# A Nyström attention and two MLP layers: the first batch's loads and the order of its scores, Newton's iteration and weight conversion

## The chip, the cores and the metric

The kernel runs on one core of a Trainium2 chip. The metric is the device time of one execution in microseconds (us). Each core has TensorE (PE in the profile, its weight loads PEld), VectorE (DVE), ScalarE (ACT), GpSimd (POOL), and SyncE (SP), which here issues all input and weight transfers.

## The reference

```python
# q, k, v: (4, 8, 576, 64) float32; 32 landmarks, each the mean of 18 consecutive tokens
q_lm = q.reshape(B, H, m, S // m, D).mean(axis=3);  k_lm likewise
A  = sm(q, k_lm)        # sm: softmax of the scaled products over the last axis
Bm = sm(q_lm, k_lm)
C  = sm(q_lm, k)
Z  = Bm^T / (norm_1(Bm) * norm_inf(Bm) + 1e-6)
for _ in range(6):
    Z = 2 * Z - Z @ Bm @ Z
x = A @ Z @ C @ v                       # per batch and head; heads side by side: (2304, 512)
g = x @ w_gate; x = (g * sigmoid(g) * (x @ w_val)) @ w_out          # 512 -> 1536 -> 512
x = (sigmoid(x @ w2_gate) * (x @ w2_val)) @ w2_out                  # the same shapes
```

## The kernel before

Four batches of 576 tokens are worked on, each in two halves g of four heads. Matmuls of the MLP run on pairs of numbers (a rounded part and the rest), so the float32 weights are loaded as raw bits (tile `raw`) and taken apart into such forms by `convert`: two passes on ACT (L329, L332) and two on DVE (L334, L338) for each piece of 128x512. The 1536 hidden columns go in six chunks c of 256. A chunk's gate and value weights of the first layer are four raw pieces, each loaded by four transfers of 128 KB; its output weights are two pieces, split by L365 and L366.

The work is written as Python generators, each `yield` a step; a scheduler sets the order of the instructions on each engine from the order in which the steps are written and from its own model of durations.

- `front(b, g)` (word F): sums each landmark's tokens (`lm`, on DVE for the very first half, on POOL in six instructions L127 to L132 for all others), turns the inputs on PE (`lt`, `tp`; copied out by ACT L141, L149), forms the landmark scores (`cs`, maximum L170, exponential `e` L175) and the 32x32 landmark matrix (`bm`, then `bs` L186, exponential L187), turns `e` (`et`, `eT` L199), multiplies with v (`cv`, L206), and last forms the scores of all tokens (`as`, L220, L221, exponential L223 into `sx`).
- `back(b)` (word B): scales `bs` by its row sums (L254), copies it into `bc` (L255), gets the norms (L258 to L273: the factor `rr`), then Newton's iteration, six products `nw` on PE with a combination on DVE between them (`rw`: first L288, then L293, L299), turns the result (`ut`, L303), and has the attention matrices normalised and turned by `a_steps` (L229 to L239, into `AH`). Up to now one step of `a_steps` follows each iteration (`step(ga)`).
- `uw_steps` (U) multiplies the converted weights `w` with `ut` (`pu`, split into `uw` by L365, L366); `gv1_steps` (G) makes the gate and value products from `AH` and `uw` (`pg`, `pv`) and `h`; `o1_steps` (O) the output products `po`.
- `load_attn` issues an input's transfer (576 KB), `load_next` that of a later half, `load_to(n)` the raw pieces up to the n-th. `wfill` is a list of weight conversions from which `emit` takes a step between the steps of other words.

The order of the start is the list of words `first`: "F00 F01 B0 I0 F10 U00 G00 F11 J0 O00 B1 ...", where F10 is `front(1, 0)`. From U00 on chunks of the MLP's first layer for batch 0 run while the other batches' attention is worked into them; the second layer follows.

Of the kernel before, what the change touches and what calls it, by code (L numbers as in the profile page):

```python
# [7 lines left out]
F32 = mybir.dt.float32  # L8
F32R = mybir.dt.float32r
U32 = mybir.dt.uint32  # L10
AF = mybir.ActivationFunctionType
ALU = mybir.AluOpType
# [4 lines left out]
def nystrom_moe_kernel(tc, q, k, v, wg1, wv1, wo1, wg2, wv2, wo2, out):  # L17
# [53 lines left out]
    def load_attn(b, which, g):  # L71
        if which == "v":
            t = att.tile([TP, 4, R, D], F32, tag="vin", name=f"vin{b}_{g}", bufs=1)
            nc.sync.dma_start(t, v[b, 4 * g:4 * g + 4].rearrange("h (p r) d -> p h r d", r=R))
        else:
            t = att.tile([P, L, D], F32, tag="in", name=f"{which}in{b}_{g}", bufs=4)
            src = {"q": q, "k": k}[which]
            nc.sync.dma_start(t, src[b, 4 * g:4 * g + 4].rearrange("h (t u) d -> (h t) u d", u=L))
        inq[which, b, g] = t
# [8 lines left out]
    def load_next(b, g, which):  # L88
        i = AORDER.index((b, g)) + (1 if which == "v" else 2)
        if i < len(AORDER):  # L90
            load_attn(AORDER[i][0], which, AORDER[i][1])
# [22 lines left out]
    def front(b, g):  # L114
# [3 lines left out]
        def sm(tag, shape, bufs=2):  # L118
            return small(tag, shape, nm_, bufs)

        def lm_steps(which):
            src = inq[which, b, g]
            lm = sm("lm", [P, 2, D], 1)
# [15 lines left out]
            bdt = sm("bd" + which, [P, 2, P], 1)  # L139
# [104 lines left out]
    def back(b):  # L244

        def sm(tag, shape, bufs=2):
            return small(tag, shape, b, bufs)
# [6 lines left out]
        nc.vector.tensor_tensor(bs, bs, bsm[:, :, None].to_broadcast([P, 2, M]), op=ALU.mult)  # L254
        nc.scalar.copy(BC[:, :, 0:M], bs)  # L255

        bmt = sm("bmt", [P, 2, M])
# [5 lines left out]
        nb = sm("nb", [P, 4, M], 1)  # L263
# [26 lines left out]
        for it in range(5):  # L290
            ps = prod(RW)
            RW2 = sm("rw", [P, 2, 96], 2)
            nc.vector.scalar_tensor_tensor(RW2, RW, 2.0, ps, op0=ALU.mult, op1=ALU.subtract)  # L293
            RW = RW2
            step(ga)
            yield
# [11 lines left out]

    for g in range(2):
        for x in "kqv" if g == 0 else "kq":  # L310
            load_attn(0, x, g)
# [34 lines left out]
    def load_in(layer, c, kk):  # L346
        t = raw_tile()
# [438 lines left out]

    def emit(word, nw=1):
# [10 lines left out]

    wfill.extend(weights(0, c) for c in range(2))
    first = (  # L800
        "F00 F01 B0 I0 F10 U00 G00 F11 J0 O00 B1 I1 U10 G10 J1 F20 O10 U01 G01 "
        "F21 U11 B2+F30 O01 G11 F31 U02 O11 G02 B3 U12 O02 G12 U03 O12 G03 U13 O03 G13"
    )
    for w in first.split():
        emit(w)
# [121 lines left out]
```

## Time and profile before

| | us |
|---|---|
| median of 3 runs (lowest, highest) | 875.0 (874.72, 875.87) |
| profiled execution, whole time | 877.74 |
| its span, first to last instruction | 876.0 |
| TensorE busy | 845.4 (97%) |
| VectorE busy | 661.2 (75%) |
| ScalarE busy | 475.4 (54%) |
| GpSimd busy | 58.8 (7%) |

The profiled execution took 1.7 us more than its span and 2.7 us more than the median. The page's chain of work that ended last gives 86% of the span to TensorE, 8% to VectorE, 3% to ScalarE and 1% to transfers. Times in a timeline are counted from the span's start.

### The profile page before, as it was taken

The page shows a single profiled execution, that of the slowest core. Times are in us where ns is not written, and L with a number is a line of the kernel's source. Part 1 is how long each engine was busy: PE and PEld are TensorE (multiplying, and loading weights), DVE is VectorE, ACT ScalarE, POOL GpSimd, SP SyncE. Part 2 cuts the span into 40 slices and gives each one's busy share as a digit, 9 for nine tenths or more (in the row PEclk, how much of TensorE's full clock was granted, in tenths as well). Part 3 has the DMA queues.
Part 4 walks back from the last instruction along what each step waited for, and adds up shares of the span by engine and source line. Part 5 has one row for each costly group of instructions (what it writes and reads, how often), then busy time and mean ns, then how long its engine had stood idle before and what let it go on. Part 6 is the DMA issues. An engine that isn't in the chain of part 4 may idle for free.

```text
span 876.0 us, 15884 instructions
## 1 busy us (share of the span) xinstructions
PE 845.4 (97%) x6172; PEld 700.8 (80%) x6172; DVE 661.2 (75%) x1295; ACT 475.4 (54%) x967; POOL 58.8 (7%) x90
## 2 busy tenths in 40 slices
PE   6788999999999999999999999999999899999998
PEld 4476777888788888888878888888888778888886
DVE  3889876866976687579998567979779965687655
ACT  5677565455752454247557655556637466455431
POOL 4635231000000000000000000000000000000000
PEclk9789999999999999999999999999999999999999
DMA  7777421021520131014614315335245433232003
GB/s 248 196 196 212 124 63 30 2 73 43 174 77 22 49 97 50 1 62 156 208 57 145 120 59 183 109 132 175 90 144 187 123 113 134 93 120 72 1 25 96
DMA packets 41484, 93.31 MB, mean 107 GB/s; under 512 B 5825, under 2 KB 8897, under 8 KB 41409
## 3 DMA queue, kind: packets, MB, share of 16 engines
q1 hardware_dynamic: 40640, 91.25, 33.4%
q10 hardware_dynamic: 768, 1.05, 0.5%
q8 instruction: 48, 0.79, 0.4%
q14 instruction: 28, 0.22, 0.1%
HBM read 72.88 MB, written 19.40 MB: 105 GB/s over the span
## 4 chain that ended last, share of the span: by engine, by line
PE 86%; DVE 8%; ACT 3%; issue 2%; DMA 1%; SPq 0%; DVEq 0%; ACTq 0%
PE po L65 31%; PE pg L65 21%; PE pv L65 20%; PE pu L65 2%; PE pgr L65 2%; PE pvr L65 2%; PE tp L148 2%; PE nw L65 1%; PE as L65 1%; PE cs L65 1%; DVE cv L334 1%; DVE acc L583 1%; DMA qin<-in_q_dram 1%; PE cv L65 1%; DVE xl L366 1%
## 5 line engine op out<-in xcount | busy, mean ns | idle before, releaser
L65 PE MATMUL po<-wo,h 128*128 128x512 f32 x432 | 109.8, 391 | 0.0
L65 PEld LDWEIGHTS po<-h,wo 128*128 128x128 f32 x480 | 82.7, 188 | 27.9 <-issue 7.5
L65 PE MATMUL po<-h,wo 128*128 128x512 f32 (+1 forms) x480 | 104.2, 373 | 0.2 <-ACT h L365 0.2
L65 PE MATMUL pg<-AH,uw 128*128 128x288 f32 x552 | 95.3, 299 | 1.3 <-ACT uw L365 1.0
L65 PEld LDWEIGHTS po<-wo,h 128*128 128x128 f32 x432 | 80.6, 188 | 17.7 <-DVE oacc L760 0.2
L65 PE MATMUL pv<-AH,uw 128*128 128x288 f32 x552 | 91.8, 297 | 0.5 <-DVE sg L525 0.5
L760 DVE TENSOR_TENSOR oacc<-po,oacc 128x512 f32<-128x512 f32 x90 | 60.0, 684 | 36.2 <-PE po L65 36.1
L65 PEld LDWEIGHTS pg<-AH,uw 128*128 128x128 f32 x552 | 80.4, 188 | 6.4 <-issue 2.5
L65 PEld LDWEIGHTS pv<-AH,uw 128*128 128x128 f32 x552 | 79.0, 188 | 4.0 <-issue 1.7
L329 ACT ACTIVATE cv<-raw 128x512 f32<-128x512 f32 x84 | 56.7, 676 | 35.2 <-DVE st L338 9.4
L65 PE MATMUL po<-hh,wo 128*128 128x288 f32 x256 | 58.9, 310 | 0.0
L334 DVE SCALAR_TENSOR_TENSOR cv<-cv,cv 128x512 uint32<-128x512 uint32 x84 | 58.0, 693 | 0.8 <-ACT cv L332 0.8
L332 ACT ACTIVATE cv<-raw 128x512 uint32<-128x512 uint32 x84 | 55.8, 669 | 3.4 <-DVE wo L366 3.4
L583 DVE TENSOR_TENSOR acc<-po,acc 128x512 f32<-128x512 f32 x64 | 43.5, 686 | 14.8 <-PE po L65 14.4
L528 ACT ACTIVATE sg<-pg 128x288 f32<-128x288 f32 x64 | 26.2, 409 | 49.5 <-PE pg L65 49.5
L65 PE MATMUL pg<-AH,wk 128*128 128x512 f32 x192 | 50.0, 390 | 0.0
L65 PE MATMUL pv<-AH,wk 128*128 128x512 f32 x192 | 49.5, 389 | 0.0
L65 PEld LDWEIGHTS po<-hh,wo 128*128 128x128 f32 x256 | 41.6, 189 | 4.8 <-issue 2.4
L365 ACT CAST h<-h 128x288 fp32r<-128x288 f32 x64 | 27.6, 433 | 30.7 <-DVE h L529 30.6
L366 DVE TENSOR_TENSOR h<-h,h 128x288 fp32r<-128x288 f32 x64 | 29.1, 456 | 17.5 <-ACT h L365 17.1
L65 PEld LDWEIGHTS pv<-AH,wk 128*128 128x128 f32 x192 | 36.0, 188 | 7.5
L65 PEld LDWEIGHTS pg<-AH,wk 128*128 128x128 f32 x192 | 35.7, 188 | 7.4 <-ACT c5g L682 0.2
(206 smaller groups left out, 1773.5 us busy)
## 6 DMA issues: line engine op xcount, KB each, us to landing
raw<-in_moe_w_out_dram SPq DMA_DIRECT2D x36, 512.0 KB, 4.1
raw<-in_moe_w_gate_dram SPq DMA_DIRECT2D x48, 128.0 KB, 3.2
raw<-in_moe_w_val_dram SPq DMA_DIRECT2D x48, 128.0 KB, 3.0
raw<-in_moe_w_gate_dram SPq DMA_DIRECT2D x24, 256.0 KB, 3.0
raw<-in_moe_w_val_dram SPq DMA_DIRECT2D x24, 256.0 KB, 3.8
wkd<-st SPq DMA_DIRECT2D x24, 256.0 KB, 3.2
wtd<-tf SPq DMA_DIRECT2D x12, 512.0 KB, 3.7
st<-wkd SPq DMA_DIRECT2D x24, 256.0 KB, 3.3
```

What stands on the lines that cost most here:

```text
L65: return nc.tensor.matmul(o, l, r, start=start, stop=stop, skip_group_check=True)
L148: nc.tensor.transpose(ps[:, j], flat(src[:, 2 * u:2 * u + 2]), ident)
L329: nc.scalar.activation(t0, hiw.bitcast(F32), AF.Copy, scale=2.0 ** -112)
L332: nc.scalar.activation(u1, low, AF.Copy, scale=0.875 * 2.0 ** -29, bias=0.49)
L334: nc.vector.scalar_tensor_tensor(u1, u0, 3, u1, op0=ALU.logical_shift_left, op1=ALU.bitwise_or)
L365: nc.scalar.copy(hi, x)
L366: nc.vector.tensor_tensor(lo, x, hi.bitcast(F32), op=ALU.subtract)
L528: nc.scalar.activation(sg, pss[0], AF.Silu)
L583: nc.vector.tensor_tensor(sl, ps, sl, op=ALU.add)
L760: nc.vector.tensor_tensor(acc, ps, acc, op=ALU.add)
```

## The change

Six things change.

1. Batch 0 is loaded in the order k0, q0, k1, raw piece 0, v0, q1, v1, raw pieces 1 to 3; all of it stands ahead of batch 1's first input. So that none of it waits for a buffer, v1 and raw piece 3 get places of the `wo` tiles, and the k side's block matrix of half 1 a place of the `CL` tiles.
2. `lm` gets two buffers.
3. Both halves' `front` are given up to before the scores of all tokens, then `back` through Newton's iteration and `ut`.
4. Twelve steps of weight conversion (chunk 0's four pieces) come next, and only then the scores of all tokens and `a_steps`; within batch 0's Newton iteration no step of `a_steps` stands any more.
5. `bc` is made by two ACT instructions that read `bs` unscaled with `bsm` as scale; `bs` is then scaled in place by two DVE instructions, which come after ACT's reading.
6. `bmt` shares the tile `nb`. The words "F00 F01 B0" leave the list.

```diff
-            t = att.tile([TP, 4, R, D], F32, tag="vin", name=f"vin{b}_{g}", bufs=1)
+            pool_, tag, bufs = (per, "wo", 2) if (b, g) == (0, 1) else (att, "vin", 1)
+            t = pool_.tile([TP, 4, R, D], F32, tag=tag, name=f"vin{b}_{g}", bufs=bufs)
...
-        if i < len(AORDER):
+        if i < len(AORDER) and (which, *AORDER[i]) not in inq:
             load_attn(AORDER[i][0], which, AORDER[i][1])
...
-            lm = sm("lm", [P, 2, D], 1)
+            lm = sm("lm", [P, 2, D])
...
-            bdt = sm("bd" + which, [P, 2, P], 1)
+            bdt = (per.tile([P, 2, P], F32, tag="CL", name="bdk01", bufs=16) if (b, g, which) == (0, 1, "k") else
+                   sm("bd" + which, [P, 2, P], 1))
...
-        nc.vector.tensor_tensor(bs, bs, bsm[:, :, None].to_broadcast([P, 2, M]), op=ALU.mult)
-        nc.scalar.copy(BC[:, :, 0:M], bs)
+        for g in range(2):
+            nc.scalar.activation(BC[:, g, 0:M], bs[:, g], AF.Copy, scale=bsm[:, g:g + 1])
+            nc.vector.tensor_scalar(bs[:, g], bs[:, g], bsm[:, g:g + 1], None, op0=ALU.mult)
...
-            step(ga)
+            if b:
+                step(ga)
...
-    for g in range(2):
-        for x in "kqv" if g == 0 else "kq":
-            load_attn(0, x, g)
...
-        t = raw_tile()
+        t = raw_tile() if (layer, c, kk) != (0, 0, 3) else per.tile([P, 2, 2 * FC], U32, tag="wo", name="raw3", bufs=2)
...
+    def advance(gen, n):
+        for _ in range(n):
+            next(gen, None)
...
+    for i, (g, x) in enumerate(((0, "k"), (0, "q"), (1, "k"), (0, "v"), (1, "q"), (1, "v"))):
+        load_attn(0, x, g)
+        if i == 2:
+            load_to(1)
+    load_to(4)
     wfill.extend(weights(0, c) for c in range(2))
     first = (
-        "F00 F01 B0 I0 F10 U00 G00 F11 J0 O00 B1 I1 U10 G10 J1 F20 O10 U01 G01 "
+        "I0 F10 U00 G00 F11 J0 O00 B1 I1 U10 G10 J1 F20 O10 U01 G01 "
...
+    f0, f1, b0 = front(0, 0), front(0, 1), back(0)
+    for gen, n in ((f0, 17), (f1, 17), (b0, 10)):
+        advance(gen, n)
+    step(wfill, 12)
+    for gen in (f0, f1, b0):
+        advance(gen, 99)
     for w in first.split():
         emit(w)
```

SyncE's queue at the program's start, before (the number ahead of the last one in a name is the half, `kin_0_123` is batch 1's first half):

```order
L78 DMA kin_0_89<-in_k_dram 128x1152
L78 DMA qin_0_91<-in_q_dram 128x1152
L74 DMA vin_0_93<-in_v_dram 96x4x384
L78 DMA kin_1_95<-in_k_dram 128x1152
L78 DMA qin_1_97<-in_q_dram 128x1152
L353 DMA raw<-in_moe_w_gate_dram 64x512
L78 DMA kin_0_123<-in_k_dram 128x1152
```

The same place after:

```order
L80 DMA kin_0_89<-in_k_dram 128x1152
L80 DMA qin_0_91<-in_q_dram 128x1152
L80 DMA kin_1_93<-in_k_dram 128x1152
L356 DMA raw<-in_moe_w_gate_dram 64x512 x2
L356 DMA raw<-in_moe_w_val_dram 64x512 x2
L76 DMA vin_0_100<-in_v_dram 96x4x384
L80 DMA qin_1_102<-in_q_dram 128x1152
L76 DMA vin_1_104<-in_v_dram 96x4x384
```

Half 1's q now comes behind raw piece 0, and between v1 and batch 1's `kin` stand twelve more transfers of raw pieces.

ACT from the exponential of half 1's landmark matrix on, before:

```order
L187 ACTIVATE bs_151,bsm_152<-bs_151 128x32
L199 COPY eT_1_363<-et_1_364 96x384
L199 COPY eT_1_363<-et_1_369 96x384
L255 COPY bc_153<-bs_151 128x2x32
L329 ACTIVATE cv_583<-raw 128x512
```

The same place after:

```order
L191 ACTIVATE bs_173,bsm_174<-bs_173 128x32
L331 ACTIVATE cv_485<-raw 128x512
L203 COPY eT_1_337<-et_1_338 96x384
L203 COPY eT_1_337<-et_1_343 96x384
L259 ACTIVATE bc_175<-bs_173,bsm_174 128x32 x2
L334 ACTIVATE cv_486<-raw 128x512
L331 ACTIVATE cv_493<-raw 128x512
```

A weight conversion's pass (L331) has come ahead of `eT`, and the two scalings into `bc` stand where one copy stood.

DVE from the nearly finished norms to Newton's first matrix, before (`L288` writes the first `rw`):

```order
L266 STREAM_TRANSPOSE nbt_460<-nb_458 128x128
L268 TENSOR_REDUCE nmax_462<-nbt_460 128x4
L206 TENSOR_SCALAR bc_153<-cv_1_374,rc_1_360 128x64
L220 TENSOR_REDUCE amx_1_403<-as_1_404 128x10
L271 TENSOR_SCALAR rr_464<-nmax_462 128x1
L221 TENSOR_TENSOR sx_1_402<-as_1_404,amx_1_403 128x320
L220 TENSOR_REDUCE amx_1_403<-as_1_428 128x8
L271 TENSOR_SCALAR rr_464<-nmax_462 128x1
L221 TENSOR_TENSOR sx_1_402<-as_1_428,amx_1_403 128x256
L273 RECIPROCAL rr_464<-rr_464 128x2
L236 STREAM_TRANSPOSE sx_0t<-sx_0_224 128x576
L288 TENSOR_TENSOR rw_477<-nw_0_468,rr_464 128x192
```

The same place after (`L293` writes the first `rw`):

```order
L336 SCALAR_TENSOR_TENSOR cv_486<-cv_485,cv_486 128x512
L269 COPY nb_383<-nrm_385 128x128
L340 SCALAR_TENSOR_TENSOR w_0_477<-cv_485,cv_486 128x512
L271 STREAM_TRANSPOSE nbt_389<-nb_383 128x128
L336 SCALAR_TENSOR_TENSOR cv_494<-cv_493,cv_494 128x512
L273 TENSOR_REDUCE nmax_391<-nbt_389 128x4
L340 SCALAR_TENSOR_TENSOR w_0_477<-cv_493,cv_494 128x512
L276 TENSOR_SCALAR rr_393<-nmax_391 128x1 x2
L224 TENSOR_REDUCE amx_0_508<-as_0_509 128x10
L278 RECIPROCAL rr_393<-rr_393 128x2
L336 SCALAR_TENSOR_TENSOR cv_502<-cv_501,cv_502 128x512
L293 TENSOR_TENSOR rw_406<-nw_0_397,rr_393 128x192
```

The scores of all tokens but one maximum have left this stretch, and five conversion passes (L336, L340) have come into it.

## Rows read from the trace of the kernel before

**Rows 1.** The page's 40 slices: granted TensorE clock, tenths of full speed.
```profile
PEclk9789999999999999999999999999999999999999
```

**Rows 2.** Busy time by stretch: PE, PEld, DVE, ACT, POOL, then PEclk, DMA share.
```profile
47.00:53.00 6.00, 5.28 (x109) 4.28 (x105) 5.15 (x15) 5.73 (x15) 0.00 (x0) 0.50 0.61 206
54.00:170.00 116.00, 112.14 (x1599) 89.33 (x1599) 94.17 (x247) 72.01 (x189) 35.31 (x50) 1.00 0.36 103
```

**Rows 3.** Timeline of SyncE's queue: start, duration, engine, line, operation, tile.
```profile
0.74 0.40 SPq L78 DMA_DIRECT2D kin<-in_k_dram  x1
...
3.37 0.56 SPq L353 DMA_DIRECT2D raw<-in_moe_w_gate_dram  x1
```

**Rows 4.** Tile views of these two transfers: from issue to landing.
```profile
DMA to landing us min/median/max: 3.7/3.7/3.7
...
DMA to landing us min/median/max: 10.5/10.5/10.5
```

**Rows 5.** Timeline of POOL, landmark sums of half 1.
```profile
11.26 1.41 POOL L127 TENSOR_TENSOR ls<-kin 128x576 f32<-128x576 f32 x1 [9.95 <-DMA kin<-in_k_dram]
...
15.15 1.42 POOL L127 TENSOR_TENSOR ls<-qin 128x576 f32<-128x576 f32 x1
...
20.05 0.60 POOL L132 TENSOR_TENSOR lm<-ls 128x64 f32<-128x64 f32 x2 [1.73 <-PE lt L138]
```

**Rows 6.** Timeline, half 1's landmark matrix to Newton's first matrix.
```profile
21.89 0.86 ACT L149 COPY kq<-tp 128x384 f32<-128x384 f32 x2
...
24.87 0.20 ACT L187 ACTIVATION_READ_ACCUMULATOR bs<-bs 128x1 f32 x1
...
25.57 0.85 ACT L199 COPY eT<-et 96x384 f32<-96x384 f32 x2 [0.51 <-PE et L198]
25.58 0.93 DVE L254 TENSOR_TENSOR bs<-bs,bsm 128x64 f32<-128x64 f32 x1
...
26.60 0.24 ACT L255 COPY bc<-bs 128x64 f32<-128x64 f32 x1 [0.18 <-DVE bs L254]
...
30.56 0.32 DVE L288 TENSOR_TENSOR rw<-nw,rr 128x192 f32<-128x192 f32 x1
```

**Rows 7.** DVE by line, 26.5 to 30.6: count, busy us, mean ns of one.
```profile
L221 DVE TENSOR_TENSOR sx<-as,amx 128x320 f32<-128x320 f32 (+1 forms) x2 | 0.9, 454 | 0.0
L220 DVE TENSOR_REDUCE amx<-as 128x10 f32<-128x320 f32 (+1 forms) x2 | 0.9, 446 | 0.0
L236 DVE STREAM_TRANSPOSE sx_0t<-sx 128x576 f32<-128x576 f32 x1 | 0.8, 759 | 0.0
```

**Rows 8.** DVE by line, 30.5 to 44.51, with idle time before.
```profile
L334 DVE SCALAR_TENSOR_TENSOR cv<-cv,cv 128x512 uint32<-128x512 uint32 x4 | 3.4, 845 | 0.0
L338 DVE SCALAR_TENSOR_TENSOR w<-cv,cv 128x512 uint32<-128x512 uint32 x3 | 2.6, 866 | 0.0
...
L229 DVE TENSOR_REDUCE asm<-sx 128x18 f32<-128x576 f32 x1 | 0.8, 753 | 1.8 <-ACT sx L223 1.8
L233 DVE TENSOR_TENSOR sx<-sx,asm 128x576 f32<-128x576 f32 x1 | 0.7, 749 | 0.0
L239 DVE TENSOR_TENSOR AH<-sx_0t,AH 128x576 fp32r<-128x576 f32 x1 | 0.7, 746 | 0.0
```

**Rows 9.** Timeline, a landmark sum on POOL beside a conversion on DVE.
```profile
36.28 1.41 POOL L127 TENSOR_TENSOR ls<-qin 128x576 f32<-128x576 f32 x1
...
36.96 1.28 DVE L338 SCALAR_TENSOR_TENSOR w<-cv,cv 128x512 uint32<-128x512 uint32 x1
```

**Rows 10.** Timeline from Newton's end to the gate and value products.
```profile
44.23 0.28 DVE L303 COPY ut<-ut 128x128 f32<-128x128 f32 x1
...
45.40 0.67 DVE L338 SCALAR_TENSOR_TENSOR w<-cv,cv 128x512 uint32<-128x512 uint32 x1
...
46.13 1.41 PE L65 MATMUL pu<-w,ut 64*32 64x512 f32 x16 [2.04 <-DVE w L338]
...
53.90 0.93 PE L65 MATMUL pg<-AH,uw 128*128 128x288 f32 x5
```

More of the change, by code (lines that the diff above doesn't have):

```diff
@@ L253, in back @@
         nc.vector.reciprocal(bsm, bsm)
-        nc.vector.tensor_tensor(bs, bs, bsm[:, :, None].to_broadcast([P, 2, M]), op=ALU.mult)
-        nc.scalar.copy(BC[:, :, 0:M], bs)
-        bmt = sm("bmt", [P, 2, M])
+        for g in range(2):
+            nc.scalar.activation(BC[:, g, 0:M], bs[:, g], AF.Copy, scale=bsm[:, g:g + 1])
+            nc.vector.tensor_scalar(bs[:, g], bs[:, g], bsm[:, g:g + 1], None, op0=ALU.mult)
+        nb = sm("nb", [P, 4, M], 1)
+        bmt = nb[:, 0:2]
         nc.vector.transpose(out=flat(bmt), in_=flat(bs))
@@ L262, in back @@
         yield
-        nb = sm("nb", [P, 4, M], 1)
         nc.vector.tensor_copy(nb, nrm.rearrange("p a b -> p (a b)")[:, :, None].to_broadcast([P, 4, M]))
```

## The prediction

> **What bounds the kernel now.** The clock row and the busy times by stretch come first [rows 1, 2]. From 54 us to 170 us TensorE is busy 112.14 of 116 us at the full clock, and the page's slices show it so to the end. There only TensorE's own work counts, and the change takes none of it away. So what the change is worth is decided before 54 us, as one question: when do the dense gate and value products of G00 begin, and how much of F10's work has been done by then? Before, their first long group starts at 53.90 [rows 10], and in 47 to 53 TensorE is busy 5.28 of 6 us, but at half its clock [rows 2]: work that is delayed into a warm stretch costs half of what it costs there.
>
> What leads to 53.90 is read backwards in the timelines. The products `pu` start at 46.13 [rows 10]; they have waited 2.04 us for the last weight conversion, which DVE did from 45.40, though `ut` was copied from 44.23 to 44.51. Newton's iteration ends there and began with `rw`, written by 30.88 [rows 6]. Ahead of that stand the exponential of half 1's `bs` (done 25.07) and the POOL sums of half 1's q, whose last row starts at 20.05 after a wait of 1.73 us for the one `lm` buffer [rows 5]. So the early chain is: landings, POOL, landmark scores, norms, Newton, `ut`, `pu`. DVE is the engine that nearly all of it shares with the weight conversion and the scores of all tokens.
>
> **The change part by part.** Times below are in the profiled execution, whose whole time of 877.74 is 2.7 above the median of 875.0; a shift of the end is carried from the one to the other unchanged.
>
> (a) Loads. The first transfer lands at 0.74 + 3.7 = 4.4, raw piece 0's first at 3.37 + 10.5 = 13.9 [rows 3, 4]. Between them landed four inputs of 576 KB and 128 KB of raw, 2432 KB in 9.4 us: 258 KB per us. By that rate half 1's q, which now has 512 KB of raw piece 0 ahead of it, lands at 4.4 + 2816/258 = 15.3 (before: 4.4 + 2304/258 = 13.3). From there the sums take as long as the k side's, 15.15 - 11.26 = 3.9 [rows 5]; k lands earlier, so POOL is free, and the second `lm` buffer takes away the wait. They end at 19.2 instead of 20.65: a gain of 1.4. SyncE's queue also moves batch 1's first input behind twelve raw transfers and v1: it lands at about 25.8, and its POOL sums run from 25.8 to 29.7. The products that read them are not due before Newton's second product, so this costs nothing by itself; without that cover it would cost F10 some 5 us. Where the sums now fall in time does cost, in (c) and (d).
>
> (b) Landmark scores of half 1. From the last sum to the end of `bs` it took 25.07 - 20.65 = 4.4. On ACT one more copy of `kq` now stands ahead of the exponentials (0.86 for two, so 0.43) [rows 6]. `bs` is done at 24.1, 1.0 earlier.
>
> (c) Scaling. Before, DVE scaled at once, 25.58 to 26.51, and ACT copied after it. Now DVE waits for ACT, which first has a conversion pass (about 0.66), the two copies `eT` (0.85) and the two scalings (0.24 each at most, by the copy of the same size) [rows 6]. Queued behind the waiting DVE are the norms and the conversions, and Newton's first product waits for both halves of `bc`. ACT is through at 26.0, DVE at 26.3 to 26.4, so the 1.0 of (b) has nearly gone. How DVE stands beside POOL bounds it from above: at 36.28 a POOL sum of 1.41 us and a DVE conversion lie side by side, and the conversion takes 1.28 [rows 9] against 0.67 at 45.40 [rows 10], where POOL is idle. Batch 1's first sum starts about 25.8, just ahead of these scalings; if it holds DVE for its 1.41 the scalings end at 27.7. I take the middle, 27.0.
>
> The Trainium skill says, on its page "SBUF — State Buffer", section "Who interferes with whom", that a VectorE instruction with two SBUF inputs and a GpSimd instruction that reads SBUF exclude each other for a whole instruction. The row at 36.96 agrees (1.28 against 0.67). By the rule alone every conversion that meets a sum would wait for what is left of it, which is the upper end in (d); the lower end is what it would be without the rule.
>
> (d) From `bs` to the first `rw`. Before it took 30.88 - 26.51 = 4.4. Out of it go the scores of half 1 and one transposition, 0.9 + 0.9 + 0.8 [rows 7], and one maximum comes in (0.45): 2.3 is left. Into it come five conversion passes on DVE of 0.67, 3.35. They lie on the path: DVE does its work in order, and the norms stand between and behind them. POOL's sums of batch 1 run beside them; by the page POOL's 58.8 us in 90 instructions are 0.65 each, so five collisions cost 0 to 3.3. I take half, 1.6, since the summing instructions differ in length and one conversion in two meets a gap. `rw` is then written at 27.0 + 2.3 + 3.35 + 1.6 = 34.2, with ends of 26.4 + 5.6 = 32.0 and 27.7 + 5.6 + 3.3 = 36.6. Before: 30.88. So Newton starts 3.3 later; this is the largest term.
>
> (e) Newton. It took 44.51 - 30.88 = 13.6. Of the six conversion passes that lay in it (0.85 to 0.87 each, 5.2) five have gone, 4.5; two subtractions into `AH` (1.5) have gone [rows 8]. In come three maxima and four subtractions of scores (3 x 0.45 + 4 x 0.45), the other half's sum and scaling (0.75 each) and two small ones (about 0.55): 5.2. The balance is -0.8 to -1.0, so 12.6. The ends are 14.6, if the exponentials of the scores on ACT are waited for as the 1.8 before L229 was [rows 8], and 10, if DVE's remaining work fits between the products better than now. `ut` is copied at 46.8 instead of 44.51, 2.3 later; all ends together, 42 to 51.
>
> (f) Weights. All of chunk 0's pieces are converted by then, so the wait of 2.04 before `pu` disappears: `pu` starts at 46.9 instead of 46.13, only 0.8 later. Late next is not `pu` but DVE behind `ut`: it has both `AH` subtractions (0.75 each), a transposition (0.76), two maxima of F10 (0.44 each), a conversion (0.67) and the first split of `uw`, about 4.1 in all, so the first products with `uw` come at 50.9.
>
> (g) To the dense stretch. By the new order on TensorE 18 of G00's products run between F10's steps, where only a few did before. F10's remainder took from about 48.0 to 53.9 at half clock; from 50.9 it takes 3.0 at full clock and 5.9 at half. With the clock full it ends at 53.9, as before, and TensorE loses nothing. By DVE it is 0 to 1.5 later, since DVE was busy 5.15 of the 6 us there [rows 2] and `ut` is 2.3 later against work of 1.8 less. I take +0.8.
>
> (h) Later batches. The new scaling and the second `lm` buffer apply to them too. From 54 us to 170 us TensorE lacks 3.9 us of being full [rows 2], and part of that lies in batch 1's iteration, so I put this at -0.5 to +0.5, and at 0.
>
> Sum: 875.0 + 0.8 = **875.8**; in the profiled execution's own terms 877.74 + 0.8 = 878.5.
>
> **The rivals.** *Newton early, faster.* If the conversions miss POOL's sums, `rw` is written at 32.0 and, with an iteration of 10 to 11, `ut` at 42 to 43, 2 earlier than before. Then neither Newton nor the weights are late, the first products come at about 47 and the start is 3 to 3.5 shorter: 872. For it: the wait of 2.04 us for weights is real and goes; against: five passes that weren't in the chain now are.
>
> *POOL holds DVE, slower.* The place is DVE between `bs` and `rw`, 26 to 36 us. Each conversion there waits for one POOL instruction, `rw` is written at 36.6 and `ut` copied at about 49: 4.5 later, of which (f) and (g) give back 0.5 to 1. That is 3.5 to 4 at the end: 879. It decides from the point at which `ut` is later than about 48.5. For it: rows 9; against: POOL's short instructions.
>
> *The clock stays low, slower.* The granted clock fell to half in 47 to 53 although TensorE was busy 5.28 of 6 us [rows 2], after a start in which it was waiting. Now its scores of all tokens have moved behind Newton, and between 26 and 34 it has little to do. If it is at half the clock when G00's products start, (g) costs 5.9 rather than 3.0: +2.9 on 875.8, some 878.5.
>
> The Trainium skill's page "TensorE: Matmul & The Clock Gate", section "What's actually happening", says that an idle TensorE falls back to the lower clock; by that alone this third rival would be the forecast. The rows show both levels before 54 us and can't say which one this order meets.
>
> *It doesn't do what it says.* If half 1's k and q come no earlier, since transfers share the engines and none is served first, (a) gives 0 instead of 1.4, and 877 results, inside the range.
>
> **How the numbers follow.** Chances: forecast 0.37 (own range 873.3 to 877.5), early Newton 0.28, POOL's hold 0.25, low clock 0.10. A measurement of this kernel can tell 0.2%, 1.75 us, from no change. Faster than 873.25 is the first rival, 0.28. Slower than 876.75 are POOL's hold, most of the low clock and the forecast's upper edge: 0.25 + 0.07 + 0.05 = 0.37. Left for the same: 0.35. For 8 in 10 the range reaches from a full gain of 4 (`ut` at 42) to the late end (`ut` near 50): 871.0 to 880.5.
>
> **What would show it.** In the profile of the changed kernel: the last sum of half 1's q ends near 19.2 without a wait for `lt` (a); `bs` is scaled by 26.4 to 27.7, released by ACT (c); five conversions lie before the first `rw`, those beside a POOL sum over 1 us long (d); `rw` at 34.2 and `ut` at 46.8; `pu` waits for `ut` and no longer for `w` (f); TensorE dense from about 54 with a full clock from 50 (g). The prediction fails if `rw` comes before 32 or after 37, if Newton takes far from 12.6, if weights are still waited for, or if a later stretch changes by more than half a us.

## The result and the profile after

| | before | after |
|---|---|---|
| median of 6 runs, same chip (lowest, highest), us | 874.64 (873.67, 875.87) | 880.82 (878.33, 882.12) |
| ratio to before (95% interval) | 1 | 1.0068 (1.0053 to 1.0084) |
| profiled execution, whole time, us | 877.74 | 882.12 |
| its span, us | 876.0 | 880.3 |

The change makes the kernel slower by about 6 us. The forecast was 875.8; the median lies 0.3 us above the upper end of the range. The profiled execution after, 882.12, is the slowest of its six, 1.3 above their median. The page of the kernel after begins with busy time, share of the span and instructions of each engine; its clock row and the chain that ended last follow.

```profile
PE 842.0 (96%) x6172; PEld 697.8 (79%) x6172; DVE 664.5 (75%) x1299; ACT 475.1 (54%) x971; POOL 59.4 (7%) x90
...
PEclk9799999999999999999999999999999999999999
...
PE 80%; DVE 10%; DMA 4%; ACT 4%; issue 2%; SPq 0%; DVEq 0%; ACTq 0%
```

TensorE is busy no longer than before (842.0 us against 845.4), so the time has gone into stretches in which it waits: its share of the chain fell from 86% to 80%. The clock row is no worse than before (9799 against 9789 in the first four slices) [rows 1].

The timeline of the kernel after, from half 1's q to Newton's first matrix (start, duration, engine, line, operation, tile, idle time before and what ended it):

```profile
17.05 1.41 POOL L129 TENSOR_TENSOR ls<-qin 128x576 f32<-128x576 f32 x1 [3.93 <-DMA qin<-in_q_dram]
...
20.26 0.59 POOL L134 TENSOR_TENSOR lm<-ls 128x64 f32<-128x64 f32 x2
...
25.39 0.23 ACT L191 ACTIVATION_READ_ACCUMULATOR bs<-bs 128x1 f32 x1
...
27.28 0.45 DVE L260 TENSOR_SCALAR bs<-bs,bsm 128x32 f32<-128x32 f32 x2 [1.28 <-ACT bc L259]
...
27.97 1.41 POOL L129 TENSOR_TENSOR ls<-kin 128x576 f32<-128x576 f32 x1 [7.12 <-DMA kin<-in_k_dram]
...
29.86 0.75 DVE L269 COPY nb<-nrm 128x128 f32<-128x128 f32 x1
...
33.39 1.40 POOL L129 TENSOR_TENSOR ls<-qin 128x576 f32<-128x576 f32 x1
33.50 1.84 DVE L336 SCALAR_TENSOR_TENSOR cv<-cv,cv 128x512 uint32<-128x512 uint32 x1
...
35.26 0.34 DVE L293 TENSOR_TENSOR rw<-nw,rr 128x192 f32<-128x192 f32 x1
```

The chain ran as described in (a) to (d), but in this execution late at its first link: POOL waited 3.93 us for half 1's q. The conversion at 33.50 took 1.84 us beside POOL's sum, against 0.67 alone [rows 10]. From Newton's end on:

```profile
46.16 1.81 POOL L129 TENSOR_TENSOR ls<-kin 128x576 f32<-128x576 f32 x1
...
46.74 0.29 DVE L309 COPY ut<-ut 128x128 f32<-128x128 f32 x1
46.95 1.63 DVE L243 TENSOR_TENSOR AH<-sx_0t,AH 128x576 fp32r<-128x576 f32 x1
...
47.25 1.09 PE L65 MATMUL pu<-w,ut 64*32 64x512 f32 x16
...
50.52 0.40 PE L65 MATMUL pg<-AH,uw 128*128 128x288 f32 x1 [1.55 <-ACT uw L368]
...
51.34 0.67 DVE L369 TENSOR_TENSOR uw<-pu,uw 128x512 fp32r<-128x512 f32 x1
...
63.68 1.43 POOL L129 TENSOR_TENSOR ls<-qin 128x576 f32<-128x576 f32 x1
63.70 1.95 DVE L340 SCALAR_TENSOR_TENSOR w<-cv,cv 128x512 uint32<-128x512 uint32 x1
...
68.79 1.18 PE L65 MATMUL cs<-kq,bdq 128*32 128x288 f32 x16 [1.07 <-ACT kq L153]
68.91 1.42 POOL L129 TENSOR_TENSOR ls<-kin 128x576 f32<-128x576 f32 x1
...
69.30 1.34 DVE L369 TENSOR_TENSOR hl<-h,hh 128x288 fp32r<-128x288 f32 x1
...
73.61 0.27 PE L65 MATMUL bm<-bdk,bdq 128*32 128x32 f32 x8 [1.32 <-ACT e L179]
```

The wait of `pu` for weights is gone. What was lost lies behind it. The copies of the output products into `acc` mark the first O00, first in the profiled kernel before, then after (count: shortest/median/longest ns, first and last start):

```profile
L565 ACT COPY acc<-po x32: 373/400/433, 61.7 to 213.0; 128x288 f32<-128x288 f32 x32
```
```profile
L568 ACT COPY acc<-po x32: 384/399/433, 69.0 to 218.3; 128x288 f32<-128x288 f32 x32
```

`ut` is 2.5 us later than before (46.74 against 44.23), the first `acc` copy 7.3, the last 5.3. So 4.8 us went between `ut` and O00. From the first to the last copy 149.3 us pass after and 151.3 before, so 2.0 of the 7.3 are regained there; from the last copy to the end of the span it takes 662.0 us after and 663.0 before.

### The profile page after: what moved, and what is told of

The parts are those of the page before. It is cut to its first block, busy times and chain, and to the rows that moved or that the text cites. A ratio compares the mean times of both kernels' runs of the same rounds, so it can differ in the third digit from the quotient of the medians.

```text
span 880.3 us, 15880 instructions
## 1 busy us (share of the span) xinstructions
PE 842.0 (96%) x6172; PEld 697.8 (79%) x6172; DVE 664.5 (75%) x1299; ACT 475.1 (54%) x971; POOL 59.4 (7%) x90
## 4 chain that ended last, share of the span: by engine, by line
PE 80%; DVE 10%; DMA 4%; ACT 4%; issue 2%; SPq 0%; DVEq 0%; ACTq 0%
PE po L65 30%; PE pg L65 19%; PE pv L65 19%; PE pu L65 2%; PE pgr L65 2%; PE pvr L65 2%; DMA vin<-in_v_dram 2%; PE nw L65 1%; PE tp L152 1%; PE as L65 1%; DVE xl L369 1%; DVE cv L336 1%; ACT cv L331 1%; DMA raw<-in_moe_w_val_dram 1%; PE cs L65 1%
## 5 line engine op out<-in xcount | busy, mean ns | idle before, releaser
L331 ACT ACTIVATE cv<-raw 128x512 f32<-128x512 f32 x84 | 56.7, 676 | 32.2 <-DVE st L340 9.4
L336 DVE SCALAR_TENSOR_TENSOR cv<-cv,cv 128x512 uint32<-128x512 uint32 x84 | 59.9, 716 | 0.8 <-ACT cv L334 0.8
L586 DVE TENSOR_TENSOR acc<-po,acc 128x512 f32<-128x512 f32 x64 | 43.5, 685 | 14.9 <-PE po L65 14.6
L369 DVE TENSOR_TENSOR h<-h,h 128x288 fp32r<-128x288 f32 x64 | 29.1, 455 | 17.4 <-ACT h L368 17.1
```

The lines of the kernel that those rows point to most:

```text
L331: nc.scalar.activation(t0, hiw.bitcast(F32), AF.Copy, scale=2.0 ** -112)
L336: nc.vector.scalar_tensor_tensor(u1, u0, 3, u1, op0=ALU.logical_shift_left, op1=ALU.bitwise_or)
L369: nc.vector.tensor_tensor(lo, x, hi.bitcast(F32), op=ALU.subtract)
L586: nc.vector.tensor_tensor(sl, ps, sl, op=ALU.add)
```

## Experiments

Ratios are to the kernel before on the same chip, with their 95% interval; 0.001 is 0.87 us. Differences between two ratios carry both intervals, combined as independent.

### What the loads cost and what the order costs, with and without POOL's sums

Two kernels each do one part: `loads_only` is before with item 1 of the change, `order_only` is after with the loads of before (items 2 to 6; raw piece 3 is back in an ordinary buffer).

```diff
 # order_only, against after
-    for i, (g, x) in enumerate(((0, "k"), (0, "q"), (1, "k"), (0, "v"), (1, "q"), (1, "v"))):
-        load_attn(0, x, g)
-        if i == 2:
-            load_to(1)
-    load_to(4)
+    for g in range(2):
+        for x in "kqv" if g == 0 else "kq":
+            load_attn(0, x, g)
```

Four more have POOL's landmark sums cut short for batches 1 to 3: `nosum_before`, `nosum_after`, `loads_no_sums` and `order_no_sums`. One short instruction takes the place of four, so a landmark is made from four tokens instead of 18 and the result is not the reference's; these kernels only serve to measure time.

```diff
-                nc.gpsimd.tensor_tensor(x, src[:, 0:NU], src[:, NU:], op=ALU.add)
 ...
-                nc.gpsimd.tensor_tensor(x[:, 0], x[:, 0], x[:, 8], op=ALU.add)
+                if b == 0:
 ...
+                else:
+                    nc.gpsimd.tensor_tensor(x[:, 0:2], src[:, 0:2], src[:, 2:4], op=ALU.add)
```

> The kernel before with the changed loads alone (order of batch 0's transfers, first weights at once, the places for them); the work is written in the old order, one lm buffer, DVE scaling. Theory 1: the loads alone move batch 1's sums later, into Newton's stretch, but bring no conversions ahead of rw unless the scheduler fills them in: 874 to 877. Rival (the loads are the cause, because batch 1's first input lands some 9 us later): 879 to 881.

> The changed kernel with the loads of before (order of transfers, raw pieces only as the steps ask for them). DVE then has the scores of all tokens where the five conversions stood. Theory 1: batch 1's sums run early again and the score instructions beside them read PSUM and only one operand from SBUF, so rw comes by 31 to 32; but the weights are converted later and pu waits for them by 2 to 4 us: 875 to 879. Rival (the order of the work alone is the cause): 880 to 882.

> The kernel before with the same four POOL instructions left out for batches 1 to 3; the order on all other engines is the same word for word. Theory 1: before had fewer collisions (1.28 and 1.09 us for conversions of 0.67), so 1 to 2 us faster than before, 873 to 874, and the two kernels without sums lie within 2 to 3 us of each other. Rival: no change, 874.6, and the two kernels without sums stay 5 to 6 us apart.

> The changed kernel with four of the six POOL instructions of each landmark sum left out for batches 1 to 3 (their landmarks are sums of four tokens instead of 18); DVE's order is the same word for word. Theory 1 (POOL's sums hold DVE in 28 to 36 us and again in 46 to 70 us): the conversions in these stretches take 0.68 us each, the first rw is written by about 33 instead of 35.6, and 4 to 6 us of the loss go: 875 to 877. Rival (the five conversions cost what they cost because they stand in DVE's order, whoever is beside them; the rest is order too): under 2 us change, 879 to 881.

> The kernel before with the changed loads alone, and four of the six POOL instructions left out of each landmark sum of batches 1 to 3. If the loads (half 1's q behind raw piece 0, landed about 17.0 instead of 13 to 14) are what keeps the two kernels without sums 2.4 us apart, this one stands with the later: 872.5 to 873.5. If the order of the work is it: 870.5 to 871.5.

> The changed kernel with the old loads, and the same POOL instructions left out. If the loads are the rest: 870.5 to 871.5. If the order is it: 873 to 876 (with sums this kernel was 5.7 above before, and its weights are converted late).

Measured, with the price of the sums as the difference of a row times 874 us:

| | with sums | without | price of the sums, us |
|---|---|---|---|
| before | 1 | 0.9953 (0.9936 to 0.9970) | 4.1 ± 1.5 |
| loads changed | 1.0021 (1.0004 to 1.0037) | 0.9948 (0.9930 to 0.9967) | 6.4 ± 2.2 |
| order changed | 1.0057 (1.0039 to 1.0076) | 1.0018 (1.0005 to 1.0031) | 3.4 ± 2.0 |
| both: after | 1.0068 (1.0053 to 1.0084) | 0.9977 (0.9960 to 0.9994) | 8.0 ± 2.0 |

Down the column with sums, the order alone costs 5.0 ± 1.6 us and the loads alone 1.8 ± 1.5, both together 5.9 ± 1.4; with the other part already in, the order costs 4.1 ± 2.0 and the loads 1.0 ± 2.1. So of the kernels that do all their sums the ones with the new order are the slow ones, and the two parts do not simply add.

The other columns say how. The sums cost more where the loads are changed, in either order: (6.4 + 8.0 - 4.1 - 3.4)/2 = 3.4 ± 2 us. Without the sums, the order costs 2.5 ± 2.2 us with the new loads (0.9977 against 0.9948) and 5.7 ± 1.9 with the old (1.0018 against 0.9953); the new loads give back 3.6 ± 1.9 under the new order and nothing measurable under the old. So the loads do two things under the new order, and these nearly cancel: they give back time and make the sums dearer. With the sums cut short on both sides, after lies 2.1 ± 2.1 us above before instead of 5.9: about 4 us of the loss (3.9 ± 2.5) hang on the sums.

What a short sum takes away is seen in the kernel after and in `nosum_after`. First two groups of DVE in the first 220 us of after (count, busy us, mean ns of one, idle before), then the same two without the sums:

```profile
L336 DVE SCALAR_TENSOR_TENSOR cv<-cv,cv 128x512 uint32<-128x512 uint32 x18 | 15.1, 839 | 0.1
L243 DVE TENSOR_TENSOR AH<-sx_0t,AH 128x576 fp32r<-128x576 f32 x4 | 4.2, 1038 | 0.0
```
```profile
L339 DVE SCALAR_TENSOR_TENSOR cv<-cv,cv 128x512 uint32<-128x512 uint32 x21 | 14.6, 695 | 0.8 <-ACT cv L337 0.8
...
L246 DVE TENSOR_TENSOR AH<-sx_0t,AH 128x576 fp32r<-128x576 f32 x4 | 3.3, 837 | 0.0
```

And its timeline:

```profile
27.10 0.35 DVE L272 COPY nb<-nrm 128x128 f32<-128x128 f32 x1
...
30.34 0.66 DVE L339 SCALAR_TENSOR_TENSOR cv<-cv,cv 128x512 uint32<-128x512 uint32 x1
30.93 0.34 DVE L296 TENSOR_TENSOR rw<-nw,rr 128x192 f32<-128x192 f32 x1
...
42.42 0.29 DVE L312 COPY ut<-ut 128x128 f32<-128x128 f32 x1
```

The last conversion before `rw` takes 0.66 instead of 1.84, the copy into `nb` 0.35 instead of 0.75, and `rw` and `ut` come 4.3 us earlier. Not all of the 4.3 is the sums': half 1's q released POOL at 14.94 in this execution and at 17.05 in that of after, so 2.1 were there before any short sum. Busy times from 46 to 70 us (PE, PEld, DVE, ACT, POOL, PEclk, DMA share, GB/s) show the stretch behind `ut`, in after and then in `nosum_after`:

```profile
46.00:70.00 24.00, 20.25 (x264) 15.40 (x262) 22.11 (x43) 18.64 (x47) 11.16 (x14) 0.93 0.54 149
```
```profile
46.00:70.00 24.00, 22.80 (x392) 19.61 (x391) 20.74 (x55) 20.34 (x56) 3.04 (x6) 1.00 0.64 182
```

In after DVE is busy 22.11 of 24 us with 43 instructions, without the sums 20.74 with 55; TensorE is busy 2.55 us less, at a lower clock. One reservation: cutting the sums short also ends POOL's own work sooner (a landmark sum takes 3.9 us [rows 5]). The price in the table is that of both, the hold on DVE (the time that a DVE instruction stands still beside POOL's) and POOL's lateness.

### Where the sums cost

`no_sums_first_half` cuts the sums short for batch 1's first half alone, `no_sums_batch1` for all of batch 1: the condition `b == 0` above becomes `(b, g) != (1, 0)` and `b != 1`.

> The changed kernel with four of the six POOL instructions left out only in the sums of batch 1's first half (28 to 37 us); DVE's order is the same. If the hold in the chain to rw is what costs, rw comes at about 33.3, 2.3 earlier, and 2 to 3 us are gained: 878 to 879. If the later holds (46 to 70 us) cost more, under 1.5 us is gained: 879.5 to 880.5.

> The changed kernel with the four POOL instructions left out of batch 1's sums only; batch 2's first sum waits for its landing near 46 us as in the changed kernel, so nothing moves into the emptied place; DVE's order is the same. If the holds of 28 to 46 us cost as much as their excess in the trace (about 3.2 us), 877 to 878.5; if only those after 46 us decide, 880 to 881.

Measured: 1.0080 (1.0063 to 1.0097) and 1.0051 (1.0037 to 1.0065). The first gave nothing, and its timeline says why:

```profile
27.68 1.52 POOL L130 TENSOR_TENSOR ls<-kin 128x576 f32<-128x576 f32 x1 [0.29 <-DMA kin<-in_k_dram]
...
27.86 1.42 DVE L272 COPY nb<-nrm 128x128 f32<-128x128 f32 x1
```

POOL's next sum, that of the second half, moved into the free place and held the copy into `nb` for 1.42 us instead of 0.35. So this run says nothing on the place. The second gives batch 1's share: 0.0017 of 0.0091, 1.5 ± 1.8 us. By that the larger part of the 8.0 us belongs to the sums of batches 2 and 3, the first of which starts at 46.16 us in after. Here too something moved up, against the expectation: batch 2's first sum began at 41.94, so batch 1's own share may be larger than this difference.

### Is it the order, because DVE stands empty early?

By the windows of 16 to 28 us, DVE is busy 2.93 of 12 us in after and 8.35 in the first profile of before (9.61 in a second one, shown below): half 0's scores of all tokens, which filled it, now come behind Newton. Part of the 2.93 is the late q of this execution; in `nosum_after` it is 4.70. `half0_scores_early` puts them back ahead, `half0_early_no_sums` does so without the sums.

```diff
-    for gen, n in ((f0, 17), (f1, 17), (b0, 10)):
+    for gen, n in ((f0, 99), (f1, 17), (b0, 10)):
```

> The changed kernel with one number changed: half 0's front is given whole, its scores of all tokens included, ahead of half 1; the conversions still come before half 1's scores. Theory 2 (DVE is what bounds the start; the change left DVE idle in 16 to 28 us, while half 1's q is summed, and put the scores that had filled this gap, some 4 to 5 us of DVE with their sums and scaling, behind the start of Newton): the gap is filled again, and 3.5 to 5 of the 6 us come back: 876 to 877.5. Theory 1 alone (POOL's hold on the conversions, which are still there): under 2 us, 879 to 881.

> Half 0's scores early and, for batches 1 to 3, four of the six POOL instructions of each landmark sum left out (sums of four tokens). If DVE's idle gap (Theory 2) and POOL's hold (Theory 1) together are the whole loss, this equals the kernel before without sums, 870.6, within 1 us. If something else in the change costs too, it stays 2 us or more above that.

Measured: 1.0043 (1.0029 to 1.0057), 2.2 ± 1.8 us better than after; without the sums 0.9985 (0.9974 to 0.9996), no better than 0.9977 (0.7 ± 1.8 us slower). So a cost of the empty stretch is measurable only together with the sums. And with half 0 early and the sums short the kernel is still 2.8 ± 1.8 us above `nosum_before` (0.9953): the empty stretch and the sums together are not the whole loss.

### Are the conversions in the wrong place?

`conversions_last` puts the twelve steps of conversion behind the scores; `half0_early_conversions_last` does both, and a third does both without the sums.

```diff
-    step(wfill, 12)
     for gen in (f0, f1, b0):
         advance(gen, 99)
+    step(wfill, 12)
```

> The changed kernel with the twelve conversion steps written behind all scores of batch 0 instead of ahead of them; DVE has score instructions where five conversions stood between bs and the first rw. Theory 2: DVE's gap of 16 to 28 stays, so the same amount of DVE work is left behind it in another order: no gain, 879.5 to 882. Theory 1: score instructions read PSUM and are not held by POOL; rw by 33, but the conversions then meet batch 1's second sums: 877 to 880.

> Both edits together: half 0's scores early, conversions behind all scores of batch 0. Theory 2: as the first run, 875 to 877.5; with Theory 1 beside it the conversions spread between Newton's products and the collisions in the chain to rw fall away: 874 to 876, near the kernel before or a little better.

> Half 0's scores early, the conversions behind all of batch 0's scores, and the same POOL instructions left out. If the conversions ahead of half 1's scores are the rest of the order's cost: 869.5 to 870.5. If not: 872 to 874.

Measured: 1.0130 (1.0113 to 1.0147), 1.0045 (1.0032 to 1.0058) and 0.9974 (0.9961 to 0.9988). In `conversions_last` the weights are late again, and TensorE falls to half its clock (timeline, then the window of 48 to 60 us):

```profile
48.88 1.96 PE L65 MATMUL pu<-w,ut 64*32 64x512 f32 x16 [4.72 <-DVE w L340]
```
```profile
48.00:60.00 12.00, 9.25 (x156) 5.92 (x156) 9.33 (x22) 7.66 (x18) 0.00 (x0) 0.50 0.21 57
```

With half 0's scores early the place of the conversions makes no measurable difference, with sums or without.

### Does the scaling on ACT, or an early Newton, decide?

`scaling_by_dve` is after with the old scaling; `half0_early_dve_scaling_no_sums` combines that with half 0 early and short sums.

```diff
-        for g in range(2):
-            nc.scalar.activation(BC[:, g, 0:M], bs[:, g], AF.Copy, scale=bsm[:, g:g + 1])
-            nc.vector.tensor_scalar(bs[:, g], bs[:, g], bsm[:, g:g + 1], None, op0=ALU.mult)
+        nc.vector.tensor_tensor(bs, bs, bsm[:, :, None].to_broadcast([P, 2, M]), op=ALU.mult)
+        nc.scalar.copy(BC[:, :, 0:M], bs)
```

> The changed kernel with bs scaled by DVE and copied by ACT, as before. The scheduler then puts the whole norm chain ahead of the conversions; only one conversion stands before the first rw, and most score work comes after ut. If the start of Newton's iteration decides (my terms c and d), rw comes near 30, ut near 42, and 3 us or more are gained: 876 to 878. If DVE's amount of work behind the gap decides (Theory 2), early Newton gains nothing since scores and AH come later: 879 to 884.

> Half 0's scores early, bs scaled by DVE as before, and four of the six POOL instructions left out of the sums of batches 1 to 3. If DVE's wait for ScalarE's scaling is the rest of the order's cost: 869.5 to 870.5. If not: 872 to 873.

Measured: 1.0091 (1.0067 to 1.0116) and 0.9969 (0.9954 to 0.9984). In `scaling_by_dve` the tile views of `rw`, `ut` and `acc` read:

```profile
L292 DVE TENSOR_TENSOR rw<-nw,rr x4: 344/352/357, 27.2 to 173.0; 128x192 f32<-128x192 f32 x4
...
L308 DVE COPY ut<-ut x4: 291/292/292, 41.2 to 183.5; 128x128 f32<-128x128 f32 x4
...
L567 ACT COPY acc<-po x32: 377/398/407, 65.7 to 215.8; 128x288 f32<-128x288 f32 x32
```

Newton starts 8 us earlier than in after and `ut` comes 5.5 us earlier; 2.6 of this is q, which released POOL at 14.48 here, and the rest goes with the conversions, which left the norms' chain. Yet the time is no better. `order_only` has an early `ut` too, but late weights behind it:

```profile
L309 DVE COPY ut<-ut x4: 280/292/292, 40.5 to 184.3; 128x128 f32<-128x128 f32 x4
```
```profile
42.82 1.96 PE L65 MATMUL pu<-w,ut 64*32 64x512 f32 x16 [2.46 <-DVE w L340]
```

`ut` at 40.5 and a ratio of 1.0057; `pu` waited 2.46 us for a conversion, and from 44 to 50 us the granted clock was 0.50. The same three moments in other profiled executions, from the tile views of `ut` and `acc` and the spans:

| | `ut` | first `acc` | between | last `acc` | span |
|---|---|---|---|---|---|
| before, first profile | 44.2 | 61.7 | 17.5 | 213.0 | 876.0 |
| before, second profile | 39.9 | 56.6 | 16.7 | 208.0 | 871.0 |
| after | 46.7 | 69.0 | 22.3 | 218.3 | 880.3 |
| scaling_by_dve | 41.2 | 65.7 | 24.5 | 215.8 | 879.5 |
| order_only | 40.5 | 65.8 | 25.3 | 215.4 | 878.2 |
| half0_scores_early | 44.0 | 61.4 | 17.4 | 211.6 | 875.5 |
| nosum_after | 42.4 | 61.1 | 18.7 | 208.2 | 871.4 |
| half0_early_no_sums | 43.8 | 58.8 | 15.0 | 208.2 | 870.0 |
| loads_no_sums | 41.1 | 57.3 | 16.2 | 204.8 | 867.8 |

Where the scores of all tokens of both halves stand behind Newton, the way from `ut` to O00 is longer, and an early `ut` is paid back there. By these rows, each of one execution, it is not when Newton ends that decides but how much is still to do behind it. The end follows the last `acc` copy at 662 to 664 us in all nine.

### Two controls on the kernel before, and the kernel before again

`two_lm_before` gives before the second `lm` buffer (and lets `bmt` share `nb`, for the place); `g00_before_f10` moves U00 and G00 ahead of F10 in addition.

```diff
-            lm = sm("lm", [P, 2, D], 1)
+            lm = sm("lm", [P, 2, D])
 ...
-        "F00 F01 B0 I0 F10 U00 G00 F11 J0 O00 B1 ...
+        "F00 F01 B0 I0 U00 G00 F10 F11 J0 O00 B1 ...
```

> The kernel before with two lm buffers alone (bmt put into the tile nb, as in the change, to make room). The sums of half 1's q end 1.7 us earlier, 18.9 instead of 20.65, and rw may come 1 to 1.7 earlier; DVE was busy 9 of 10 us in 20 to 30, so if DVE bounds the start (Theory 2) it gives 0 to 1: 873.5 to 875. If the chain of landings and sums bounds it: 1.5 to 2 faster, 872.5 to 873.

> The kernel before with two lm buffers and with U00 and G00 written ahead of F10. If VectorE's work ahead of the dense stretch bounds the start, F10's scores leave it: 1 to 3 us faster than before, 871 to 873. If TensorE then lacks F10's transposes and scores to fill its waits in Newton and G00: 1 to 3 us slower.

> The kernel before once more, for the profile of a common execution: the one profiled first took 877.74, 2.7 above its median, with a mean granted clock of 0.988, while most of its executions show 0.992 to 0.994 and spans of 871 to 873. If the surplus is the half-clock stretch of 46.8 to 53.6 us, this trace shows the full clock there and G00's long groups from about 51 instead of 53.90; if it lies elsewhere, that stretch is at half clock again and the span still near 872.

Measured: 1.0001 (0.9992 to 1.0010), 1.0011 (0.9995 to 1.0027) and, for before against itself, 1.0014 (0.9998 to 1.0030). The buffer changes nothing measurable. Nothing that was run beats the kernel before while doing all of its sums.

The second profile of before is the more useful part. First the window of 48 to 54 us in the profile that the forecast rests on, then in the second one:

```profile
48.00:54.00 6.00, 5.74 (x138) 5.19 (x138) 4.86 (x13) 4.73 (x12) 0.00 (x0) 0.53 0.54 168
```
```profile
48.00:54.00 6.00, 6.00 (x72) 5.91 (x61) 6.00 (x15) 3.75 (x10) 2.28 (x3) 1.00 1.00 243
```

And the second profile's timeline and `acc` copies:

```profile
28.88 0.32 DVE L288 TENSOR_TENSOR rw<-nw,rr 128x192 f32<-128x192 f32 x1
...
39.92 0.29 DVE L303 COPY ut<-ut 128x128 f32<-128x128 f32 x1
...
48.32 0.93 PE L65 MATMUL pg<-AH,uw 128*128 128x288 f32 x5
...
L565 ACT COPY acc<-po x32: 384/399/424, 56.6 to 208.0; 128x288 f32<-128x288 f32 x32
```

The same program has a full clock where the first profile has 0.53 (its own half-clock stretch came earlier: 0.54 from 40 to 46 us), `ut` 4.3 us and the dense products 5.6 us earlier, and a span of 871.0 us instead of 876.0. Neither profile is the middle one: of the 119 executions of before that were timed beside these runs the median is 873.84, two took 877.7 or more and 15 took 872.8 or less.

## Why the prediction was wrong, step by step

**The basis.** The text carried a shift of the end "from the one to the other unchanged". That step failed. The profiled execution, 877.74 us, was among the slowest of a kernel whose median is 874.6; its mean granted clock was 0.988, and it met half clock just where (g) needed it. The second execution, at 0.994, has no half clock from 48 to 54 us. Every "before" that ends in rows 2, 6, 8 and 10 is later than in that execution: `rw` by 1.7 us, `ut` by 4.3, the dense products by 5.6.

**(a)** Measured against the wrong row. In the trace of after, half 1's q was issued at 5.32 and released POOL at 17.05, not 15.3; POOL's sums ended at 20.85, not 19.2. But that trace is the latest of thirteen profiled executions with the new loads: in them the first sum of q began between 13.75 and 17.05, in ten before 15.0, and in those ten the sums ended between 18.2 and 19.1. Two lines, from `nosum_after` and `no_sums_batch1`:

```profile
14.94 1.76 POOL L130 TENSOR_TENSOR ls<-qin 128x576 f32<-128x576 f32 x1 [2.89 <-DMA qin<-in_q_dram]
```
```profile
13.75 1.41 POOL L130 TENSOR_TENSOR ls<-qin 128x576 f32<-128x576 f32 x1 [2.08 <-DMA qin<-in_q_dram]
```

So 15.3 was not too early. What was not there is the gain: it was counted from 20.65, and in the second profile of before the sums end at 18.96. This is the rival "It doesn't do what it says". Nor is a late q the cause of the loss: in `no_sums_first_half` it released POOL at 14.39, and the median was 880.91.

**(b), (c), (d)** Right in the main. From the last sum to `bs` 25.62 - 20.85 = 4.8 (4.8 forecast); scaled at 27.73, inside 26.4 to 27.7 but for 0.03, released by ACT after a wait of 1.28; five conversions before `rw`, written at 35.60, inside 32.0 to 36.6. In (c) the forecast gave batch 1's first sum half a hold on the scalings; it began only at 27.97, behind them, and from `bs` to the scaled `bs` took 2.1 us instead of 2.9. From the scaling to `rw` 7.9 us against 7.25.

The forecast took half of the largest possible hold, 1.6; by the rows it was 33.50's 1.84 - 0.67 = 1.2, the copy into `nb` 0.75 - 0.22 = 0.5, and a smaller one at 28.98 (0.95 - 0.67 = 0.3): 2.0 in all. The Trainium skill, page "SBUF — State Buffer", section "Who interferes with whom", says that a VectorE copy can, under conditions, take the shared port pair too, and not only an instruction with two SBUF inputs. The rows agree: the copy into `nb` reads one input; its median is 0.22 us in after and 0.23 in before, and beside POOL it took 0.35, 0.75 and 1.42 in three kernels. The forecast counted conversions only.

**(e)** Inside its ends. Newton took 47.03 - 35.60 = 11.4 (12.6 forecast, ends 10 and 14.6), and `ut` was copied at 47.03 (46.8). That this is so near is partly luck: the chain was 1.5 us late at `bs`, 0.7 at the scaling, 1.4 at `rw` and 0.2 at `ut`, as misses of both signs met.

**(f)** Right for the weights: `pu` started at 47.25 without a wait for `w` (46.9). Mis-sized for the work behind `ut`, which is where the loss begins. From the end of `ut` to the end of DVE's first split the forecast put 4.1 us; it took 52.01 - 47.03 = 5.0, and the same seven instructions 4.0 in `nosum_after` (42.71 to 46.67). The sum at 46.16 held the subtraction at 46.95, which took 1.63 us against 0.78 there. The products at 50.52 (50.9 forecast) had only ACT's part of `uw`; the next ones waited for the split until 52.07.

**(g)** The step that failed most. It had F10's remainder end at 53.9 and the dense stretch 0.8 us later than before. F10's last scores ended at 58.8 and the first long group of G00 came at 58.76, 4.9 later than 53.90 (10.4 later than the 48.32 of before's second profile), though 18 of G00's products had run by then, as forecast. The first `acc` copy came 7.3 later, the last 5.3.

First, TensorE waited, and nothing in the step allowed for it. In after it was busy 3.56 of the 6 us from 47 to 53, and then worked without a pause at a lower clock (the windows 47 to 53 and 54 to 60):

```profile
47.00:53.00 6.00, 3.56 (x39) 1.59 (x33) 6.00 (x11) 4.36 (x10) 3.20 (x4) 1.00 0.54 180
```
```profile
54.00:60.00 6.00, 6.00 (x143) 5.58 (x142) 4.44 (x10) 4.05 (x11) 0.00 (x0) 0.77 0.18 40
```

Second, DVE's work behind `ut` was taken as a fixed amount, and nothing was said of what would hold it. Batch 2's sums ran at 46.16, 63.68 and 68.91. The first is told under (f); beside the second the conversion at 63.70 took 1.95 us, beside the third the split at 69.30 took 1.34 (others 0.46), and TensorE waited 1.07 us for `kq` and 1.32 for `e`. Before, the sum that corresponds to that of 63.68 hit nobody. In the second profile of before:

```profile
58.04 1.53 POOL L127 TENSOR_TENSOR ls<-qin 128x576 f32<-128x576 f32 x1
...
60.33 0.46 DVE L170 TENSOR_REDUCE cmx<-cs 128x1 f32<-128x288 f32 x1 [2.05 <-PE cs L65]
```

DVE stood idle from 58.28 to 60.33 for TensorE, just while POOL ran; in the first profile likewise (idle 2.10 before 65.48, the sum at 63.64). In after DVE is busy 3.85 of the 4 us from 62 to 66, and so the same sum has become a wait. Third, the step gave back 2.9 us by going from half to full clock. That gain exists only against the execution in which before had half clock.

**(h)** Outside its ends, and not where the time went. From the first to the last `acc` copy after took 149.3 us, before 151.3 and 151.4 in its two profiles: 2.0 less, not 0 ± 0.5. What was not costed at all is the later batches' sums. The price of all sums rose by 3.9 ± 2.5 us (8.0 - 4.1), and batch 1's account for only 1.5 ± 1.8 of the 8.0. By the traces the rise lies ahead of O00, in (g)'s stretch: behind the first `acc` copy the sums cost 149.3 - 147.1 = 2.2 us after and 2.7 before (second profile against `nosum_before`).

**The rivals.** "POOL holds DVE, slower" named what about 4 of the 5.9 us hang on. Its place was too narrow, since it put all of the hold between `bs` and `rw`, where it amounted to 2.0 us, and so was the point from which it decides: `ut` came at 47.0, before 48.5, and the kernel was slower than the 879 given. "Newton early" holds only where POOL is out of the way: in `nosum_after` `ut` came at 42.4 and the time was 873.0, near its 872; with `ut` at 41.2 and the sums in place, `scaling_by_dve` took 881.4. "The clock stays low" was wrong at the point named, where G00's first products start (1.00 from 50 to 52), but right three us later: after TensorE's waits the granted clock fell to 0.50 from 54 to 56, while it worked off F10. At 0.77 over the 6 us from 54 to 60 this took about 1.4 us (an estimate from the row above). It came with the waits, and no run separates the two.

**What stays open.** Which part of the order costs the 2.5 ± 2.2 us that remain without the sums, and how the 5.0 ± 1.6 of the order with the old loads divides into its late weights, the half clock and the rest. Taking the scaling back to DVE (0.9969) or the conversions behind the scores (0.9974), each with half 0's scores early, comes nearer to the 0.9948 of `loads_no_sums`, but the intervals of all of these overlap. Also open is how the price of the sums divides into hold on DVE and lateness of POOL.

## What to carry to other kernels

Before costing a change to a start, compare the profiled execution's time and clock with the median of the runs, and take no term from a stretch at half clock, and no landing time, unless a second execution shows it too. A load that is put later moves everything that its arrival starts: list the POOL work behind it, and look at which DVE instructions that work will then stand beside, on to the batches that the change does not name. An earlier end of the critical chain is worth only what the work behind it can use at once: here Newton's end moved by 5.5 us, about 3 of them by the change in the kernel, with no gain.

## What was not expected of the hardware

- The granted clock of the same program differed between executions: profiles of the kernel before have a mean of 0.988 and 0.994, with spans of 876.0 and 871.0 us, and the difference is there by the first `acc` copy (61.7 against 56.6 us).
- A DVE copy with one input took 0.22 us as a rule and 1.42 beside a POOL sum of 1.52. A conversion took 0.66 alone; one that began 0.11 us after a sum of 1.40 took 1.84, and waiting out the 1.29 that was left of the sum and then running would make 1.95: it stood still for nearly all of it.
- The same transfer, half 1's q with the same loads ahead of it, released POOL's first sum at 17.05 in one execution (after) and between 13.75 and 16.32 in twelve others with the new loads, though nothing that differs between after and `nosum_after` (14.94) runs before that.
